# Channel groups of 28 contiguous channels, an output stored in two parts, and the D term on GpSimd, in an SSM kernel

## Chip, cores, metric

One core of one Trainium2 chip. The metric is device microseconds (us) of one execution; each kernel is timed in rounds beside the kernel before on the same chip. Profiles are of one execution; their span is some 1.8 us shorter than the time.

## The reference, cut to what matters

```python
x = A_u                                               # (1, 2048, 448), bf16
g = sigmoid((x * gate_w).sum(-1, keepdims=True))
a = S4(x)    # causal convolution of length 2048 with K[d,l] = Re sum_n C dB exp(dt A l), plus x * Dskip
b = x * (causal_conv(kv, ssm_k) + kv * ssm_D)         # kv = shift_conv(k) * v
return g * a + (1 - g) * b                            # (1, 2048, 448), bf16
```

Both convolutions are done as Fourier-like stages of small matmuls. The output is 2048 tokens of 448 channels; in memory one token is a row of 896 bytes.

## The kernel before

The 448 channels lie as 4 quarters (on partition groups of 32) of 112. A quarter is worked in four groups H = 0 to 3. Before, a group was 2 x 14 channels: 14 from each half of the quarter. Eight filter blocks (two for each group) build the S4 kernel K: products on VectorE, then 224 small matmuls into `pk`, an eviction `kg_S` (a copy out of the matmuls' accumulators by ScalarE), a gather, a spread. The products that the matmuls read are `kg_TP` and `kg_TQ`. All sums gather in `ug`, a tile of 128 x 64 x 112.

```python
def sk_cols(H, raw=None):                      # filter of B: D goes into its first tap
    raw = load_sk(H) if raw is None else raw   # 8 DMAs, one for each quarter and half
    s0 = raw[:, :, :, 0]
    V.tensor_tensor(out=s0, in0=s0, in1=dB[:].rearrange(...)[:, H * NW:(H + 1) * NW, :], op=ALU.add)
    return lambda h, w: raw[:, w, h, :]
...
def epilogue_B(H):                             # two multiplications of 448, one for each half
    ...
    for h in range(2):
        V.tensor_tensor(out=o[:, :, :, h], in0=pv[:, :, :, h], in1=o[:, :, :, h], op=ALU.mult)
...
def epilogue_A(H):
    ...
    V.tensor_tensor(out=o, in0=t, in1=o, op=ALU.add)           # the last sum of this group
    if H == NQG - 1:                                           # after the last group: whole rows
        for g in range(4):
            dmae[g % 2].dma_start(out4[g][:, b0:b0 + n, :], ug[g * 32:(g + 1) * 32, b0:b0 + n, :])
```

With halves interleaved, three finished groups were three times 14 columns at two places. So the output went out at the very end in whole quarter rows, 112 channels or 224 bytes at a time.

## Time and profile before

| | before |
|---|---|
| time, median of 3 | 339.62 us (339.61 to 339.71) |
| span of the profile | 338.0 us |
| last filter block's matmuls begin | 303.40 us |
| last sum on VectorE ends | 328.71 us |
| from there to the end ("tail") | 9.3 us |

The lines that carry this are in the prediction below. The view of the DMA queues in the stretch from 324 to 345 us (queue, packets, MB, share of 16 engines) shows the final stores:

```profile
q10 hardware_dynamic: 4224, 0.92, 26.9%
q1 hardware_dynamic: 4224, 0.92, 25.4%
```

From this comes a figure used throughout: 52.3% of 16 engines for 21 us, over 8448 packets, is **20.8 ns of packet time per packet** of 224 bytes. (A packet of the output is one run of contiguous bytes in a row: 2048 x 4 = 8192 of them, and 256 more.) It adds up the packets' own times. Where the engines are full these overlap, and the share passes 100% (119.6% from 329 to 335 us); the interval between two packets of an engine is then shorter, here 6 us x 16 / 5484 packets = 17.5 ns. And the timeline of TensorE (PE) in the last filter block (start, us, what, count, idle time before):

```profile
303.40 2.89 PE L367 MATMUL pk<-kg_TP,kg_TQ 128*21 128x32 bf16 x181
307.15 0.84 PE L367 MATMUL pk<-kg_TP,kg_TQ 128*21 128x32 bf16 x43 [0.87 <-issue]
```

The block's 224 matmuls are broken by a pause of 0.87 us for which the profile knows no releaser ("issue").

### The profile page before, as it was taken

To read this page: it belongs to the slowest core of one execution; us is meant where nothing else is said; L and a number is where in the kernel's file an instruction comes from. 1 tells how busy PE (TensorE), PEld (TensorE's weight loads), DVE (VectorE), ACT (ScalarE), POOL (GpSimd) and SP (SyncE) were. 2 spreads that over 40 slices of the span, in tenths; PEclk is the share of its full clock that TensorE was granted. 3 is DMA by queue.
4 is the path that set the end of the run, shared out by engine and by line. 5 is a ranking of instruction groups with operands and counts; after the bars stand their busy time and mean duration, and the time that the engine had idled before them with its cause. 6 is when DMAs were issued, how large, how long until landed. Compare 5 with 4: busy or idle time off the path is not lost.

```text
span 338.0 us, 12004 instructions
## 1 busy us (share of the span) xinstructions
PE 226.8 (67%) x5294; PEld 199.9 (59%) x5294; DVE 284.6 (84%) x610; ACT 237.5 (70%) x375; POOL 14.9 (4%) x132
## 2 busy tenths in 40 slices
PE   0098326686287448758897975997977769966740
PEld 0033226565286347748886864996966658965740
DVE  5799499798997999999979999796999999982440
ACT  4524368988996069997998998769889565942620
POOL 8700000000000000000000000000000000000000
PEclk9999677578559676987999995899878759977595
DMA  8899994422804000032004004100400120040039
GB/s 136 121 154 192 163 146 100 67 82 78 155 2 111 2 4 1 6 83 72 2 4 112 3 4 110 43 5 2 112 0 5 42 70 4 4 111 6 0 72 147
DMA packets 53803, 21.40 MB, mean 63 GB/s; under 512 B 49208, under 2 KB 52088, under 8 KB 53752
## 3 DMA queue, kind: packets, MB, share of 16 engines
q1 hardware_dynamic: 49064, 19.47, 31.6%
q10 hardware_dynamic: 4368, 1.03, 1.9%
q8 instruction: 41, 0.67, 0.8%
q0 software_dynamic: 320, 0.15, 0.3%
q14 instruction: 10, 0.08, 0.1%
HBM read 10.09 MB, written 3.21 MB: 39 GB/s over the span
## 4 chain that ended last, share of the span: by engine, by line
ACT 33%; PE 24%; DVE 19%; SPq 11%; DMA 7%; issue 4%; DVEq 0%; ACTq 0%
ACT zs L560 11%; PE ps_b L274 5%; PE pk L367 5%; ACT zsK L560 5%; PE ps_a L260 4%; PE ps_c L208 4%; ACT ET L479 4%; ACT U L560 4%; SPq L613 3%; DVE kg_P L313 2%; SPq L618 2%; ACT ET L491 2%; PE ps L221 2%; DMA modes<-in_A_C_im_dram 2%; ACT ks_mag L479 2%
## 5 line engine op out<-in xcount | busy, mean ns | idle before, releaser
L313 DVE TENSOR_TENSOR kg_P<-kg_TQ,ET 128x896 bf16<-128x896 bf16 (+1 forms) x64 | 43.8, 705 | 0.4
L221 PEld LDWEIGHTS <-s_W 128*128 128x128 bf16 x480 | 33.3, 117 | 17.5 <-issue 15.2
L560 ACT CAST zs<-ps_c 128x1024 bf16<-128x1024 f32 (+1 forms) x48 | 42.4, 936 | 0.6 <-PE ps_c L208 0.5
L560 ACT CAST zs<-ps 128x896 bf16<-128x896 f32 x48 | 40.9, 924 | 0.3 <-PE ps L221 0.2
L221 PE MATMUL ps<-zs,s_W 128*128 128x112 bf16 x384 | 31.0, 248 | 12.2 <-ACT zs L560 6.4
L260 PE MATMUL ps_a<-sa_R,zs 128*128 128x128 bf16 x196 | 30.4, 246 | 10.0 <-ACT zs L560 8.0
L491 ACT ACTIVATE ET<-ks_ph 128x448 bf16<-128x448 int16 x40 | 23.6, 604 | 16.2 <-DVE ks_ph L487 16.0
L560 ACT CAST zsK<-ps_c 128x512 bf16<-128x512 f32 (+2 forms) x30 | 25.6, 856 | 13.1 <-PE ps_c L208 13.1
L560 ACT CAST U<-ps_a 128x1024 bf16<-128x1024 f32 (+2 forms) x32 | 29.7, 948 | 4.9 <-PE ps_a L260 2.8
L367 PE MATMUL pk<-kg_TP,kg_TQ 128*21 128x32 bf16 x1792 | 29.4, 238 | 4.8 <-issue 3.8
L260 PEld LDWEIGHTS <-zsS 128*128 128x128 bf16 x196 | 26.8, 153 | 8.4 <-issue 8.1
L367 PEld LDWEIGHTS <-kg_TQ 128*21 128x21 bf16 x1792 | 27.6, 121 | 6.2 <-issue 5.6
L313 DVE TENSOR_TENSOR kg_P<-kg_TP,ET 128x1792 bf16<-128x1792 bf16 (+1 forms) x32 | 30.9, 965 | 0.0
L260 PE MATMUL ps_a<-sa_R,zsS 128*128 128x128 bf16 x196 | 30.2, 246 | 0.6 <-issue 0.6
L274 PE MATMUL ps_b<-U,sb_G 128*128 128x28 bf16 x1024 | 27.9, 177 | 3.4 <-ACT U L560 1.3
L274 PEld LDWEIGHTS <-sb_G 128*128 128x128 bf16 x1024 | 27.6, 98 | 4.1 <-issue 4.0
L661 PE MATMUL ps_v<-kvt,scratch 128*128 128x448 bf16 x64 | 17.1, 405 | 18.3 <-DVE kvt L657 17.9
L260 PEld LDWEIGHTS <-zs 128*128 128x128 bf16 x196 | 26.9, 153 | 3.4 <-DVE zs L281 2.0
L318 DVE TENSOR_TENSOR kg_TQ<-kg_P 128x896 bf16<-128x896 bf16 (+2 forms) x64 | 27.6, 441 | 0.2
L208 PE MATMUL ps_c<-WcK,kg_KT 128*64 128x128 bf16 x224 | 19.9, 303 | 10.3 <-ACT zsK L560 7.8
L208 PEld LDWEIGHTS <-kg_KT 128*64 128x64 bf16 x224 | 17.3, 209 | 12.1 <-issue 8.7
L661 PEld LDWEIGHTS <-scratch 128*128 128x128 bf16 x64 | 6.8, 108 | 28.1 <-issue 18.9
(138 smaller groups left out, 476.7 us busy)
## 6 DMA issues: line engine op xcount, KB each, us to landing
zsS<-zs SPq DMA_DIRECT2D x16, 448.0 KB, 4.4
kt<-in_B_k_dram SPq DMA_DIRECT2D x8, 224.0 KB, 5.9
vt<-in_B_v_dram SPq DMA_DIRECT2D x4, 448.0 KB, 8.2
skraw<-in_B_ssm_k_dram SPq DMA_DIRECT2D x32, 56.0 KB, 2.7
uu<-in_A_u_dram SPq DMA_DIRECT2D x4, 448.0 KB, 6.8
xfd<-ks_hold SPq DMA_DIRECT2D x2, 672.0 KB, 3.0
ks_xf<-xfd SPq DMA_DIRECT2D x3, 336.0 KB, 3.0
out_dram<-ug SPq DMA_DIRECT2D x8, 112.0 KB, 4.5
```

Source lines behind the costliest of these rows:

```text
L208: nc.tensor.matmul(pt[64 * r:64 * r + 64, i, :], lhsT=x, rhs=W[:, 128 * r:128 * r + 128], start=True, stop=True, tile_position=(0, 64 * r))
L221: nc.tensor.matmul(pt[:, i // 4, (i % 4) * n:(i % 4 + 1) * n], lhsT=W[:, k].rearrange("p r s -> p (r s)"), rhs=zs[:, k], start=True, stop= ...
L260: nc.tensor.matmul(pt[:, i, :], lhsT=t[:].rearrange("p k (g c) -> p (k g) c", g=4)[:, :, j + i], rhs=R[:, 128 * n:128 * n + 128], start=(n ...
L274: nc.tensor.matmul(o, lhsT=G[:, b, r].rearrange("p g a -> p (g a)"), rhs=U[:, r, b], start=(r == 0), stop=(r == 1))
L313: put(V.tensor_tensor(out=P4[:, i:i + m].rearrange("p n v c m -> p n v (c m)"), in0=in0, in1=in1, op=ALU.mult))
L318: put(V.tensor_tensor(out=T[:, dst:dst + v.shape[1] // 2].rearrange("p n v m -> p (n v) m"), in0=v[:, :, 0], in1=v[:, :, 1], op=ALU.add))
L367: nc.tensor.matmul(pt[32 * g:32 * g + NQ, hw, :].rearrange("p (i j) -> p i j", i=2), lhsT=TQ[:, :, c, m], rhs=rhs, start=(hf == 0 and c == 0),
L479: ex = nc.scalar.activation(dst, x, ACT.Exp, scale=float(e))
L491: sn = nc.scalar.activation(dst.rearrange("p b c m -> p b (c m)"), low16(ph[:].rearrange("p b c m -> p (b c m)")).rearrange("p (b x) -> p ...
L560: nc.scalar.copy(dst, src)
L613: nc.sync.dma_start(kt[g * 32:(g + 1) * 32, 3 + b0:35 + b0, :], k4[g][:, b0:b0 + 32, :])
L661: nc.tensor.matmul(pt[:, i, 0:448], lhsT=ident, rhs=t[:, n, 4 * i:4 * i + 4, :].rearrange("p b l -> p (b l)"), start=(n == 0), stop=(n == 3))
```

## The change

Its intent: a group is now 28 contiguous channels of a quarter. So three groups are columns 0 to 83, which can be stored while the last filter block is still being made, and only a quarter of the output is left for the end. Contiguous groups also make one operation of two in B's epilogue, and four DMAs of eight for the filter. The D term moves from VectorE to GpSimd, and priorities are set anew. Core of the diff:

```diff
     def sk_cols(H, raw=None):
         raw = load_sk(H) if raw is None else raw
-        s0 = raw[:, :, :, 0]
-        V.tensor_tensor(out=s0, in0=s0, in1=dB[:].rearrange("p (h v) -> p v h", h=2)[:, H * NW:(H + 1) * NW, :], op=ALU.add)
+        nc.gpsimd.tensor_tensor(out=raw[:, :, 0], in0=raw[:, :, 0], in1=dB[:, H * NC:(H + 1) * NC], op=ALU.add)
 ...
     def epilogue_B(H):
-            for h in range(2):
-                V.tensor_tensor(out=o[:, :, :, h], in0=pv[:, :, :, h], in1=o[:, :, :, h], op=ALU.mult)
+            V.tensor_tensor(out=o, in0=pt.rearrange("p i (b c) -> p i b c", b=16), in1=o, op=ALU.mult)
+    def store(b0, n, c0, c1):
+        for g in range(4):
+            dmae[g % 2 if c1 == 112 else 0].dma_start(out4[g][:, b0:b0 + n, c0:c1], ug[g * 32:(g + 1) * 32, b0:b0 + n, c0:c1])
     def epilogue_A(H):
+            if H == NQG - 2:
+                store(b0, n, 0, 3 * NC)
             if H == NQG - 1:
-                for g in range(4):
-                    dmae[g % 2].dma_start(out4[g][:, b0:b0 + n, :], ug[...])
+                store(b0, n, 3 * NC, 112)
 ...
-        with tc.high_priority(offset=200000):      # gather and spread of a filter block
+        with tc.high_priority(offset=100):
 ...
-        U = stage_a(nc, psum, qp, R, terms[c], evac)
+        with tc.high_priority(offset=300000):
+            U = stage_a(nc, psum, qp, R, terms[c], evac)
-        with tc.high_priority(offset=300000):      # stage B; the same for the products
+        with tc.high_priority(offset=200000):
```

(NC is 28, so 3 * NC is 84.)

More of the change, by code (lines that the diff above doesn't have):

```diff
@@ L21 @@
 HALF = 32768.0
-NV = 56
 NQG = 4
-NW = NV // NQG
-CW = 7
-NBLK = NV // CW
-M = 16 * CW
+NC = 112 // NQG
+CB = NC // 2
+NBLK = 2 * NQG
+M = 8 * CB
 NMODE = 896
@@ L199, in col_of, with spread @@
         return self.sel[:, self.var[key]].rearrange("p a b -> p (a b)")
-def spread(nc, psum, W, zs, cols, groups, evac, room=8, tag="ps", order=None):
+def spread(nc, psum, W, zs, cols, groups, evac, room=8, tag="ps", at=0):
     for whs in groups:
@@ L210, in spread @@
         n = len(whs)
-        at = order.index(whs[0]) if order else whs[0]
-        evac(zs[:].rearrange("p k (g c) -> p (k g) c", g=4)[:, :, at:at + n], pt[:, 0:n].rearrange("p i kg -> p kg i"))
+        evac(zs[:].rearrange("p k (g c) -> p (k g) c", g=4)[:, :, at + whs[0]:at + whs[0] + n], pt[:, 0:n].rearrange("p i kg -> p kg i"))
 def transform(nc, psum, W, zs, evac, ks=range(4)):
-    n = 8 * NW
+    n = 4 * NC
     for kk in ks:
@@ L238, in transform_half @@
             k0 = 16 * kk + 8 * i
-            evac(half_of(zs, k0, k0 + 8, half), pt[:, i, 0:448].rearrange("p (k c) -> p k c", c=NW), i)
+            evac(half_of(zs, k0, k0 + 8, half), pt[:, i, 0:448].rearrange("p (k c) -> p k c", c=CB), i)
 def stage_a_half(nc, psum, U, R, terms, evac, half):
-    for h in range(2):
+    for j in range(half * CB, half * CB + CB, 7):
         pt = psum.tile([P, 8, 128], f32, name="ps_a", tag="ps")
-        for i in range(CW):
+        for i in range(7):
             for n, t in enumerate(terms):
-                nc.tensor.matmul(pt[:, i, :], lhsT=t[:].rearrange("p k (g c) -> p (k g) c", g=4)[:, :, half * NW + h * CW + i],
+                nc.tensor.matmul(pt[:, i, :], lhsT=t[:].rearrange("p k (g c) -> p (k g) c", g=4)[:, :, j + i],
                                  rhs=R[:, 128 * n:128 * n + 128], start=(n == 0), stop=(n == 1))
-        j = h * NW + half * CW
-        evac(U[:, :, :, j:j + CW].rearrange("p r b c -> p (r b) c"), pt[:, 0:CW].rearrange("p i rb -> p rb i"))
+        evac(U[:, :, :, j:j + 7].rearrange("p r b c -> p (r b) c"), pt[:, 0:7].rearrange("p i rb -> p rb i"))
 def stage_a(nc, psum, pool, R, terms, evac):
-    U = pool.tile([P, 2, 64, 2 * NW], bf16, name="U", tag="q")
-    for j in range(0, 2 * NW, 8):
-        m = min(8, 2 * NW - j)
+    U = pool.tile([P, 2, 64, NC], bf16, name="U", tag="q")
+    for j in range(0, NC, 8):
+        m = min(8, NC - j)
         pt = psum.tile([P, 8, 128], f32, name="ps_a", tag="ps")
@@ L271, in stage_b @@
             b = b0 + i
-            o = pt[:, i // 16, (i % 16) * 2 * NW:(i % 16 + 1) * 2 * NW]
+            o = pt[:, i // 16, (i % 16) * NC:(i % 16 + 1) * NC]
             for r in range(2):
@@ L358, in block @@
             pt = self.pk[:, 0:448].rearrange("p (n b) -> p n b", b=32)
-            for hw in range(2 * CW):
-                h, w = divmod(hw, CW)
+            for hw in range(CB):
                 for hf in range(2):
@@ L363, in block @@
                         for g in range(4):
-                            m = ((hf * 4 + g) * 2 + h) * CW + w
+                            m = (hf * 4 + g) * CB + hw
                             r0 = TP[:, 0, c, m:m + 1]
@@ L369, in block @@
                                              stop=(hf == 1 and c == 1), tile_position=(0, 32 * g))
-            S = self.pool.tile([P, 32, 2 * CW], bf16, name="kg_S")
-            evac(S[:].rearrange("p b n -> p n b"), pt) if False else evac(S[:], pt.rearrange("p n b -> p b n"))
+            S = self.pool.tile([P, 32, CB], bf16, name="kg_S")
+            evac(S[:], pt.rearrange("p n b -> p b n"))
         return S
@@ L375, in gather @@
         nc, cons = self.nc, self.cons
-        KT = self.pool.tile([P, 64, 2, CW], bf16, name="kg_KT")
+        KT = self.pool.tile([P, 64, CB], bf16, name="kg_KT")
         for r in range(8):
@@ L401, in gather @@
             if r == 0:
-                for h in range(2):
-                    v0 = h * NV + j * CW
-                    jobs.append((0, o[0:32, 0, h * CW:(h + 1) * CW], self.sel_d[:], self.d4[:, v0:v0 + CW]))
+                jobs.append((0, o[0:32, 0, :], self.sel_d[:], self.d4[:, j * CB:(j + 1) * CB]))
             for a0 in range(4):
@@ L411, in gather @@
             if r % 4 == 3:
-                evac(KT[:].rearrange("p (b r) h w -> p r b (h w)", r=8)[:, r - 3:r + 1], pt[:, 0:448].rearrange("p (r b n) -> p r b n", r=4, b=8))
+                evac(KT[:].rearrange("p (b r) n -> p r b n", r=8)[:, r - 3:r + 1], pt[:, 0:448].rearrange("p (r b n) -> p r b n", r=4, b=8))
         return KT
@@ L429, in scaled @@
         for i, t in enumerate(self.hold):
-            nat = lambda ap: ap.rearrange("p f (x b w) -> p f x b w", x=8, w=CW)[:, :, :, 4 * i:4 * i + 4]
+            nat = lambda ap: ap.rearrange("p f (g b w) -> p f g b w", g=4, w=CB)[:, :, :, 4 * i:4 * i + 4]
             dtv = self.dt[:].unsqueeze(1).to_broadcast([P, 2, 448])
-            self.nc.vector.tensor_tensor(out=dst(t).rearrange("p b (f x w) -> p f x b w", f=2, w=CW), in0=nat(src), in1=nat(dtv), op=ALU.mult)
+            self.nc.vector.tensor_tensor(out=dst(t).rearrange("p b (f g w) -> p f g b w", f=2, w=CB), in0=nat(src), in1=nat(dtv), op=ALU.mult)
     @staticmethod
@@ L575, in hqt @@
         return qp.tile(shape, dtype, name=name, tag="hq", bufs=NBH)
-    sk_src = B_ssm_k.rearrange("(g h v) (a b) -> g h a v b", g=4, h=2, a=32)
+    sk_src = B_ssm_k.rearrange("(g c) (a b) -> g a c b", g=4, a=32)
     def load_sk(H):
-        raw = hqt([P, NW, 2, 64], "skraw")
+        raw = hqt([P, NC, 64], "skraw")
         for g in range(4):
-            for h in range(2):
-                nc.sync.dma_start(raw[g * 32:(g + 1) * 32, :, h, :], sk_src[g, h][:, H * NW:(H + 1) * NW, :])
+            nc.sync.dma_start(raw[g * 32:(g + 1) * 32], sk_src[g][:, H * NC:(H + 1) * NC, :])
         return raw
@@ L587, in sk_cols, with spread_in @@
         raw = load_sk(H) if raw is None else raw
-        s0 = raw[:, :, :, 0]
-        V.tensor_tensor(out=s0, in0=s0, in1=dB[:].rearrange("p (h v) -> p v h", h=2)[:, H * NW:(H + 1) * NW, :], op=ALU.add)
-        return lambda h, w: raw[:, w, h, :]
-    halves = [h * NW + s * CW + w for s in range(2) for h in range(2) for w in range(CW)]
-    def spread_in(cols, order=None):
-        zs = qt([P, 32, 8 * NW], "zs")
-        groups = [(order or list(range(2 * NW)))[j:j + 8] for j in range(0, 2 * NW, 8)]
-        spread(nc, psum, Wc, zs, lambda wh: cols(*divmod(wh, NW)), groups, evac, order=order)
+        nc.gpsimd.tensor_tensor(out=raw[:, :, 0], in0=raw[:, :, 0], in1=dB[:, H * NC:(H + 1) * NC], op=ALU.add)
+        return lambda c: raw[:, c, :]
+    def spread_in(cols):
+        zs = qt([P, 32, 4 * NC], "zs")
+        spread(nc, psum, Wc, zs, cols, [list(range(j, min(j + 8, NC))) for j in range(0, NC, 8)], evac)
         return zs
@@ L601, in with_swap @@
         transform(nc, psum, W2, zs, evac)
-        swap = qt([P, 32, 8 * NW], "zsS")
+        swap = qt([P, 32, 4 * NC], "zsS")
         for r in range(2):
@@ L671, in body @@
     for H in range(NQG):
-        q = lambda t: t.rearrange("p b (h v) -> p b h v", h=2)[:, :, :, H * NW:(H + 1) * NW]
-        kvq.append(hqt([P, 64, 2, NW], "kv"))
+        q = lambda t: t[:, :, H * NC:(H + 1) * NC]
+        kvq.append(hqt([P, 64, NC], "kv"))
         kvl = V.tensor_tensor(out=kvq[H][:], in0=q(vt[:]), in1=q(kt[:, 3:67]), op=ALU.mult)
@@ L708, in block @@
         if KA[H] is None:
-            KA[H] = qt([P, 32, 8 * NW], "zsK")
+            KA[H] = qt([P, 32, 4 * NC], "zsK")
         S = kg.block(j, evac, kvl if j == 0 else None)
-        with tc.high_priority(offset=200000):
+        with tc.high_priority(offset=100):
             KT = kg.gather(j, S, evac)
-            w0 = (j % 2) * CW
-            groups = [[h * NW + w0 + w for w in range(CW)] for h in range(2)]
-            cols = lambda wh: KT[:, :, wh // NW, wh % NW - w0]
+            at = (j % 2) * CB
+            cols = lambda c: KT[:, :, c]
@@ L716, in block @@
             if j == NBLK - 1:
-                spread(nc, psum, WcK, KA[H], cols, groups, evac, order=halves)
+                spread(nc, psum, WcK, KA[H], cols, [range(0, 7), range(7, 14)], evac, at=at)
             else:
-                spread(nc, psk, WcK, KA[H], cols, [x for q in groups for x in (q[0:4], q[4:])], evac, 4, "ps_g",
-                       halves if H == NQG - 1 else None)
+                spread(nc, psk, WcK, KA[H], cols, [range(0, 4), range(4, 8), range(8, 11), range(11, 14)], evac, 4, "ps_g", at)
@@ L722, in window @@
     def window(b0, n, H):
-        return ug[:, b0:b0 + n, :].rearrange("p (i b) (h v) -> p i b h v", b=16, h=2)[:, :, :, :, H * NW:(H + 1) * NW]
+        return ug[:, b0:b0 + n, H * NC:(H + 1) * NC]
     def epilogue_B(H):
         def consume(b0, n, pt):
-            o = window(b0, n, H)
-            pv = pt.rearrange("p i (b h w) -> p i b h w", b=16, h=2)
-            for h in range(2):
-                V.tensor_tensor(out=o[:, :, :, h], in0=pv[:, :, :, h], in1=o[:, :, :, h], op=ALU.mult)
-        return consume
+            o = window(b0, n, H).rearrange("p (i b) c -> p i b c", b=16)
+            V.tensor_tensor(out=o, in0=pt.rearrange("p i (b c) -> p i b c", b=16), in1=o, op=ALU.mult)
@@ L733, in epilogue_A @@
+        return consume
+    def store(b0, n, c0, c1):
+        for g in range(4):
+            dmae[g % 2 if c1 == 112 else 0].dma_start(out4[g][:, b0:b0 + n, c0:c1], ug[g * 32:(g + 1) * 32, b0:b0 + n, c0:c1])
     def epilogue_A(H):
         def consume(b0, n, pt):
-            t = kgp.tile([P, 2, 16, 2, NW], bf16, name="ept")
-            t = t[:, 0:n // 16]
-            V.tensor_tensor(out=t.rearrange("p i b h w -> p i b (h w)"), in0=pt.rearrange("p i (b x) -> p i b x", b=16),
-                            in1=gt[:, b0:b0 + n].rearrange("p (i b) -> p i b", b=16).unsqueeze(3).to_broadcast([P, n // 16, 16, 2 * NW]), op=ALU.mult)
@@ L739, in consume @@
-            o, t = [x.rearrange("p i b h w -> p (i b) h w") for x in (window(b0, n, H), t)]
-            V.tensor_tensor(out=o, in0=t, in1=o, op=ALU.add)
+            t = kgp.tile([P, 32, NC], bf16, name="ept")[:, 0:n]
+            V.tensor_tensor(out=t.rearrange("p (i b) c -> p i b c", b=16), in0=pt.rearrange("p i (b c) -> p i b c", b=16),
+                            in1=gt[:, b0:b0 + n].rearrange("p (i b) -> p i b", b=16).unsqueeze(3).to_broadcast([P, n // 16, 16, NC]), op=ALU.mult)
+            V.tensor_tensor(out=window(b0, n, H), in0=t, in1=window(b0, n, H), op=ALU.add)
@@ L741, in consume @@
+            if H == NQG - 2:
+                store(b0, n, 0, 3 * NC)
             if H == NQG - 1:
-                for g in range(4):
-                    dmae[g % 2].dma_start(out4[g][:, b0:b0 + n, :], ug[g * 32:(g + 1) * 32, b0:b0 + n, :])
+                store(b0, n, 3 * NC, 112)
         return consume
     def kv_cols(H):
-        return lambda h, w: kvq[H][:, :, h, w]
+        return lambda c: kvq[H][:, :, c]
     def u_cols(H):
-        return lambda h, w: uu[:, :, h * NV + H * NW + w]
+        return lambda c: uu[:, :, H * NC + c]
@@ L757, in step @@
         else:
-            XA[H] = spread_in(u_cols(H), halves if H == NQG - 1 else None)
-        U = stage_a(nc, psum, qp, R, terms[c], evac)
+            XA[H] = spread_in(u_cols(H))
+        with tc.high_priority(offset=300000):
+            U = stage_a(nc, psum, qp, R, terms[c], evac)
         if kind == "B":
@@ L764, in step @@
             XA[H] = with_swap(XA[H])
-        with tc.high_priority(offset=300000):
+        with tc.high_priority(offset=200000):
             stage_b(nc, psum, G, U, (epilogue_A if c[0] == "A" else epilogue_B)(c[1]))
         if kind == "B":
-            with tc.high_priority(offset=300000):
+            with tc.high_priority(offset=200000):
                 terms[n] = products(nc, *KB[H], XB[H])
@@ L774, in step @@
             transform(nc, psum, W2, KA[H], evac)
-            with tc.high_priority(offset=300000):
+            with tc.high_priority(offset=200000):
                 terms[n] = products(nc, *XA[H], KA[H])
@@ L797, in body @@
         step(seq[j], seq[j + 1], j)
-    U = qt([P, 2, 64, 2 * NW], "U")
+    U = qt([P, 2, 64, NC], "U")
     def last(half):
```

## The prediction

> **What bounds the kernel now.** I read the page's busy table and its row of slices first, then the waits of VectorE (DVE), then the chain that ended last in order of time, and last the timeline of the end.
>
> ```profile
> PE 226.8 (67%) x5294; PEld 199.9 (59%) x5294; DVE 284.6 (84%) x610; ACT 237.5 (70%) x375; POOL 14.9 (4%) x132
> ...
> DVE  5799499798997999999979999796999999982440
> ACT  4524368988996069997998998769889565942620
> ```
>
> DVE is at nine tenths or more in nearly every slice up to about 304 us. Its few idle gaps are these (engine and line waited for: us in total, times, longest):
>
> ```profile
> DVE ept L737 <- PE ps_b L274: 7.9, 4, 4.5
> DVE ET L503 <- ACT ET L491: 6.8, 4, 3.0
> DVE skraw L589 <- DMA skraw<-in_B_ssm_k_dram: 6.7, 2, 4.3
> ```
>
> So the kernel has three parts. Up to about 90 us, loads and DVE alternate, with 6.7 us in which DVE stands in front of its own 28-element add (the D term) because the filter's load has not landed. From 90 to 303 us DVE is nearly full, but after 196 us the chain of waits no longer names it: it runs over ACT evictions and PE, so DVE and the PE-ACT pair are both close to the bound. From 303.4 us on, all is one serial chain (last filter block, gather, spread, transform, two stages, output). The chain (start, us, what) and the end of the timeline:
>
> ```profile
> 29.67 7.12 DMA modes<-in_A_C_im_dram
> 36.81 3.23 DMA skraw<-in_B_ssm_k_dram
> ...
> 62.15 2.90 DMA skraw<-in_B_ssm_k_dram
> 65.72 1.85 DVE ks_tC_im L456
> ```
>
> ```profile
> 325.27 7.69 SPq L743 DMA_DIRECT2D out_dram<-ug  x8
> 325.28 8.10 ACTq L743 DMA_DIRECT2D out_dram<-ug  x8
> ...
> 328.32 0.39 DVE L740 TENSOR_TENSOR ug<-ept,ug 128x448 bf16<-128x448 bf16 x1
> ```
>
> The last arithmetic ends at 328.71 and the span at 338.0: 9.3 us are output stores alone.
>
> **What the Trainium skill says.** (1) "DMA: Bandwidth & Descriptors", section "Why small descriptors are slow (HBM only)": each packet carries a fixed overhead on the engine's internal bus, beside its 32-byte beats, and fixed descriptor metadata. The trace agrees in kind: in windows with the 16 DMA engines full, 128-byte packets ran at 119 GB/s (36 to 37 us), 224-byte ones at 155 (28 to 29) and 512-byte ones at 234 (34 to 35), which is 17, 23 and 35 ns per packet and engine. A straight line through these has some 11 ns at zero bytes: a 56-byte packet costs an estimated 14 ns, not a quarter of 23. (2) "VectorE: DVE Perf Modes", section "Why PSUM operands drop a tier": a float32 PSUM operand goes at one element per cycle. Agrees: 896 elements from PSUM took 1086 ns (L737), 448 took 616 (L730), so a fixed part of about 146 ns. (3) "GPSIMD Engine Reference", section "Key points": GpSimd shares its SBUF interfaces with VectorE and is about half as fast at elementwise work. No two-input GpSimd operation is in this trace, so nothing here shows it. (4) "ScalarE: Activation LUTs", section "What ACT_TABLE_LOAD costs": about 1283 ns for the load. Agrees: 1283 ns in every row of table loads, 13 of them.
>
> **The change, part by part.**
>
> *D added on GpSimd.* Four DVE adds go: 4 x 0.284 = 1.1 us. The wait is another matter. The second of the two waits (2.37 us at 63.1, in front of L456) should vanish: in the changed order DVE has ks_tC_im next, whose PSUM operand was written by 60.3. The first (4.30 us at 36.0) should not. In the changed order of instructions GpSimd's first add stands in front of three of the four sb_j iotas, and DVE's next operation needs the second iota, which in the kernel before was made at 14.07, long ahead. So the new wait is load, add, iota (0.62 us each in the timeline), then DVE. The load itself is a little earlier: before, the eighth skraw DMA waited for a transfer slot that modes C_im freed at 36.79, after which 3.23 us passed, and in 38 to 39 us the DMA share fell to 0.71; now four DMAs of twice the size need slots freed sooner. The bytes stay behind the same modes bytes, so I take 0.5 us off the landing at 40.04. Then an add (0.5 us, an estimate from GpSimd's 0.2 us for small memsets and 0.65 for iotas) and an iota: sb_ph starts near 40.8 instead of 40.41. The new order also has only one of two phases ahead of the first four mask products, which delays the second sine; I count +1.0 us for this stage in all.
>
> *Epilogue of B in one piece.* 16 instructions of 616 ns become 8 of 1086 (the same shape as L737 now): 9.9 - 8.7 = 1.2 us less on DVE.
>
> *Order around the gate.* The changed order on ACT has 12 table loads instead of 13: the sine that stood after the gate's sigmoid is now before it. Before, DVE waited 1.69 us at 84.7 for just that sine: -1.7 us.
>
> *Priorities.* Stage A goes ahead of the gather, the gather behind. The order on PE and DVE is otherwise close to the old one, and PE's tail after the last filter block is the same. One place looks worse: before the last block, the second-to-last block's spread had 8 of its 28 matmuls ahead of stage B (292.05), now all 28 follow it. They go through one PSUM buffer, and a round of matmul and eviction took 1.5 to 1.7 us there (297.06, 298.45, 300.21). One more round after stage B, less about 0.8 us that stage A gains by not being broken up: +0.8 us, on the path to the last block's matmuls.
>
> *Smaller things.* One D-skip matmul per block instead of two (8 fewer, 0.2 us each at most), half as many skraw DMAs at the same packets: nothing on the path.
>
> *Output.* Columns 0 to 83 go out after the third A epilogue, whose sums ended at 299.7 and 302.8. Eight DMAs on the SP queue with 1024 packets each, 8192 x 20 ns / 16 = 10 us from 300: landed near 313, behind nothing that matters (the last swap was issued at 296), 12 us before the queue is needed. The final stores keep their 16 DMAs and 8192 packets, but of 56 bytes. Before: 512 packets per engine, from 325.6 to about 336.7, 21.7 ns each: DMA-bound. Now 512 x 14 = 7.2 us if full, and the sums that feed them come every 1.15 us until 328.7, so at best the last four DMAs start at 329 and land in the 2.9 us that the fastest store took. I take the last landing at 332.5 instead of 337: -4.5 us. This is the largest and surest term.
>
> **Sum.** DVE before the last block: +1.0 - 2.4 - 1.1 - 1.2 - 1.7 = -5.4 us. Since the chain after 196 us runs over ACT and PE, I let 60% of it through: -3.2. Spread order: +0.8. Stores: -4.5. In all -6.9: 339.6 - 6.9 = 332.7, I say 332.6.
>
> **The rivals.**
> 1. *The stores cost by the packet, not the byte.* The final part has as many packets as before; if a 56-byte write costs HBM as much as a 224-byte one, the tail stays at 9 us and the result is about 337. Against it: reads show 17 ns at 128 bytes and 23 at 224. For it: no store below 224 bytes is in the trace.
> 2. *PE and ACT are the bound after 90 us.* Then the DVE savings come back as DVE idle time, and only stores and some of the start remain: 339.6 - 4.5 + 0.8 - 1 = 335. For it: the chain after 196 us. Against: DVE had under 6 us of idle time between 130 and 303.
> 3. *DVE savings come through in full and the new priorities clear PE and ACT waits* (stage A sooner means U, stage B and buffers sooner): -5.4 - 4.5 and 1 or 2 more: 328.5. For it: eviction and PE waits of 8 to 13 us in total (kg_S, zsK, ps_a) that priorities can move.
> 4. *GpSimd holds things up*: its add could be blocked by DVE's two-input work, or its wait in front of the iotas be longer than I count. Then the start loses 2 or 3 us and the result is near 335.5. Slower than before by 2% would need a stall of 13 us, and nothing in the order points to one.
>
> **Range and chances.** The stores may give 1 to 5.5, DVE 1 to 6, priorities -2 to +2, the start -1 to +2; combined about 3 us to each side, a little more upwards: 328.5 to 337. The 2% line is 332.8, just about my value; the priorities look tuned for this layout, which tips it a little: 0.52 faster, 0.46 within, 0.02 slower.
>
> **What would show it.** Right: the time from the last DVE sum to the end is 5 us or less; no DVE wait on a skraw DMA, but one of 4 to 5 us on GpSimd's iota near 36 us; DVE near 281 us busy; 12 table loads; the last block's matmuls (pk) start some 2 us earlier than 303.4. Wrong: final stores still taking 9 us (rival 1); DVE idle between 90 and 300 us grown by the 3 to 4 us that it saved (rival 2); DVE waiting more than 6 us for GpSimd (rival 4).

## The result

The changed kernel took **344.19 us** in the median of 4 runs (343.67 to 345.17), the kernel before in the same rounds 339.66 (339.61 to 340.61). The ratio is 1.013, 95% interval 1.010 to 1.016: slower, by less than the 2% line. Ratios here are the mean time of one kernel's fast runs over that of the other's fast runs of the same rounds, so not quite the ratio of the medians quoted.

The busy row of the page after (busy us, share, instructions):

```profile
PE 224.7 (66%) x5286; PEld 196.2 (57%) x5286; DVE 284.6 (83%) x598; ACT 233.1 (68%) x374; POOL 16.9 (5%) x136
```

VectorE has 12 instructions fewer and is busy for the same 284.6 us. The last sum in the timeline after:

```profile
328.50 0.39 DVE L727 TENSOR_TENSOR ug<-ept,ug 128x448 bf16<-128x448 bf16 x1
```

The last sum ends at 328.50 + 0.39 = 328.89, where before it ended at 328.71: the arithmetic is no faster. The tail is 342.1 - 328.89 = 13.2 us, where before it was 9.3. A quarter of the bytes takes 3.9 us longer, nearly the whole difference of the spans (4.1). The DMA queues from 324 to 345 us:

```profile
q10 hardware_dynamic: 4224, 0.23, 45.5%
q1 hardware_dynamic: 4224, 0.23, 35.8%
```

The same 8448 packets, a quarter of the megabytes, and 81.3% x 16 x 21 us / 8448 = **32.3 ns per packet**. The prediction had 14, as an interval between packets of full engines; measured in that way it is 8 us x 16 / 4327 packets = 29.6 ns (330 to 338 us). The early store, whose packets of 168 bytes are the only large traffic between 298 and 318 us, shows the same:

```profile
q1 hardware_dynamic: 8322, 1.38, 81.1%
```

81.1% x 16 x 20 us / 8322 = 31.2 ns per packet, more than the 20.8 of the longer 224 bytes.

These are means of two very different stretches. Two views of one microsecond each, from 327 and from 329 us:

```profile
q1 hardware_dynamic: 722, 0.04, 41.2%
q10 hardware_dynamic: 632, 0.03, 33.3%
```

```profile
q10 hardware_dynamic: 387, 0.02, 144.8%
q1 hardware_dynamic: 280, 0.02, 68.0%
```

So the first packets of 56 bytes took 8.8 ns each (74.5% x 16 us / 1354), and two microseconds later 51.0 (212.8% x 16 us / 667). The early store does it too (17 ns a packet from 299 to 301 us, 30 to 54 from 302 to 309), and so do the misaligned stores of split_72 and split_76 below, each after some 2300 to 3400 packets; the aligned ones do not (split_80 has 9.2, 10.5, 11.0, 11.0 and 12.2 ns in the five microseconds from 327). Why, no run shows. And TensorE in the last filter block:

```profile
301.17 3.12 PE L363 MATMUL pk<-kg_TP,kg_TQ 128*21 128x32 bf16 x191
307.24 0.71 PE L363 MATMUL pk<-kg_TP,kg_TQ 128*21 128x32 bf16 x33 [2.96 <-issue]
```

The block starts 2.2 us earlier than before, as predicted ("some 2 us earlier than 303.4"), but its pause has grown from 0.87 to 2.96 us. So the block ends where it did, and the eviction that follows starts at 308.00 where it was 308.03. (The start of this block varies: in seven later kernels with the same order of arithmetic it lay between 301.9 and 304.6, in one execution each, so these 2.2 us are not a sure gain either.)

Two of the waits of VectorE after, both near the start (us in total, times, longest):

```profile
DVE sb_ph L87 <- POOL sb_j L138: 3.6, 1, 3.6
DVE sb_G L147 <- ACT sb_v L144: 3.6, 2, 2.8
```

No wait for skraw is left: both, 6.7 us, are gone. New are 3.6 us for GpSimd's iota and more waits for the sine behind it. The timeline of GpSimd shows why:

```profile
39.60 0.32 POOL L581 TENSOR_TENSOR skraw<-skraw,dB 128x28 bf16<-128x28 bf16 x1 [25.55 <-DMA skraw<-in_B_ssm_k_dram]
39.80 1.14 POOL L138 IOTA sb_j<- 128x512 int32 x2
43.33 0.77 POOL L138 IOTA sb_j<- 128x512 int32 x1 [2.38 <-DVE sb_ph L87]
```

The add waits for the load, and the iotas, of which two wait for nothing, stand behind it. The k-v product starts at 51.62, 2.8 us later than before (48.80); 0.8 us of these were lost before the add (VectorE's `kvt` products start at 17.12, before at 16.28). The gains that follow (no second skraw wait, no wait for a table load) just make up for it: the first filter block's products start at 89.61, before at 89.74.

Two suspects, then: what the two stores do (tail and pause), and why nothing else in the change gained.

### The profile page after: what moved, and what is told of

Its sections match the earlier page's. It is cut to its first block, busy times and chain, and to the rows that moved or that the text cites. A ratio compares the mean times of both kernels' runs of the same rounds, so it can differ in the third digit from the quotient of the medians.

```text
span 342.1 us, 11970 instructions
## 1 busy us (share of the span) xinstructions
PE 224.7 (66%) x5286; PEld 196.2 (57%) x5286; DVE 284.6 (83%) x598; ACT 233.1 (68%) x374; POOL 16.9 (5%) x136
## 3 DMA queue, kind: packets, MB, share of 16 engines
HBM read 10.09 MB, written 3.21 MB: 39 GB/s over the span
## 4 chain that ended last, share of the span: by engine, by line
ACT 33%; PE 27%; DVE 19%; SPq 10%; issue 4%; DMA 3%; DVEq 0%; POOL 0%; ACTq 0%; POOLq 0%
ACT zs L554 11%; PE pk L363 8%; PE ps_b L271 6%; PE ps_c L207 5%; ACT zsK L554 5%; PE ps_a L257 4%; ACT U L554 4%; ACT ET L473 3%; SPq L602 3%; ACT ET L485 2%; SPq L607 2%; ACT ks_mag L473 2%; DVE kg_P L310 2%; PE ps L219 2%; SPq L613 2%
## 5 line engine op out<-in xcount | busy, mean ns | idle before, releaser
L219 PEld LDWEIGHTS <-s_W 128*128 128x128 bf16 x480 | 30.8, 110 | 19.3 <-issue 17.1
L363 PE MATMUL pk<-kg_TP,kg_TQ 128*21 128x32 bf16 x1792 | 29.6, 238 | 13.3 <-DVE kg_TP L320 8.3
L219 PE MATMUL ps<-zs,s_W 128*128 128x112 bf16 x384 | 28.9, 234 | 14.2 <-ACT zs L554 9.0
L554 ACT CAST U<-ps_a 128x1024 bf16<-128x1024 f32 (+2 forms) x32 | 28.9, 940 | 6.5 <-PE ps_a L257 4.6
L554 ACT CAST zsK<-ps_c 128x512 bf16<-128x512 f32 (+2 forms) x30 | 22.5, 756 | 13.2 <-PE ps_c L207 13.2
L650 PE MATMUL ps_v<-kvt,scratch 128*128 128x448 bf16 x64 | 17.8, 414 | 19.0 <-DVE kvt L646 18.7
```

Source lines behind the costliest of these rows:

```text
L219: nc.tensor.matmul(pt[:, i // 4, (i % 4) * n:(i % 4 + 1) * n], lhsT=W[:, k].rearrange("p r s -> p (r s)"), rhs=zs[:, k], start=True, stop= ...
L363: nc.tensor.matmul(pt[32 * g:32 * g + NQ, hw, :].rearrange("p (i j) -> p i j", i=2), lhsT=TQ[:, :, c, m], rhs=rhs, start=(hf == 0 and c == 0),
L554: nc.scalar.copy(dst, src)
L650: nc.tensor.matmul(pt[:, i, 0:448], lhsT=ident, rhs=t[:, n, 4 * i:4 * i + 4, :].rearrange("p b l -> p (b l)"), start=(n == 0), stop=(n == 3))
```

## The experiments

Twelve kernels ran, in three groups on one chip each, all but shift_fetch in rounds with the kernel before. "Cut" is the column at which the output is divided between early and final store. Since a quarter row begins at a multiple of 224 bytes in rows of 896 bytes, both multiples of 32, a run is aligned to 32 bytes exactly if twice the cut is a multiple of 32. (In the built program `ug` lies at byte 29,984 of each partition, a multiple of 32 too. So a cut is aligned or not on both sides at once, in on-chip memory where the store reads and in HBM where it writes, and no run here tells the two apart.)

### 1. No early store: late_store

```diff
-            if H == NQG - 2:
-                store(b0, n, 0, 3 * NC)
-                store(b0, n, 3 * NC, 112)
+                store(b0, n, 0, 112)
```

> The changed kernel without the early store; the final stores carry all 112 channels (224-byte runs) again. The order of instructions on PE, DVE and GpSimd is the changed kernel's. Theory A (short misaligned runs make the final stores slow: 13.2 us from the last sum to the end, against 9.3 before): the tail goes back to 9.3. Theory B (the early store's 8192 packets hold up PE's instruction fetch, which is the 2.96 us gap in the last block's pk matmuls): the gap falls to about 1 us, so the last sum comes 2 us earlier, near 326.8. A and B: span 336, 338 us in time. A without B: span 338.2, time 340. Rival (the tail is long because the queue's transfer slots are still held by the early store): tail 9.3 here too, told apart by early_and_full.

Measured: 339.91 us (338.38 to 341.47), ratio to before 0.9995 (0.9951 to 1.0039). Last sum at 329.42, tail 9.4 us, and the pause:

```profile
303.57 3.06 PE L363 MATMUL pk<-kg_TP,kg_TQ 128*21 128x32 bf16 x191
307.92 0.71 PE L363 MATMUL pk<-kg_TP,kg_TQ 128*21 128x32 bf16 x33 [1.29 <-issue]
```

What follows: the whole loss is the divided store. And all the rest of the change (grouping, GpSimd, one-piece epilogue, priorities) is worth nothing in sum, within 0.5% either way; gains and losses may cancel in it.

### 2. Early store kept, and whole rows at the end: early_and_full

```diff
-                store(b0, n, 3 * NC, 112)
+                store(b0, n, 0, 112)
```

The result is the same (columns 0 to 83 are written twice with the same values).

> The changed kernel with its early store kept, and the final stores again of all 112 channels, so that 84 are written twice with the same values. Theory A (run length or alignment): tail 9.3 us from the last sum, as before the change. Rival (the early store's slots or its traffic make the tail long): tail stays near 13. Theory B (instruction fetch behind the early store): the gap of some 3 us in the last pk matmuls stays, last sum near 328.9. So A and B: span 338.2, time 340; rival: time 344.

Measured: 342.25 us, ratio 1.006 (1.0021 to 1.0098). Tail 9.4 us. The order of the instructions on every compute engine is that of late_store, yet the last sum ends at 331.49, 2.07 us later:

```profile
303.92 3.24 PE L363 MATMUL pk<-kg_TP,kg_TQ 128*21 128x32 bf16 x183
307.55 0.40 PE L363 MATMUL pk<-kg_TP,kg_TQ 128*21 128x32 bf16 x8 [0.39 <-issue]
310.00 0.71 PE L363 MATMUL pk<-kg_TP,kg_TQ 128*21 128x32 bf16 x33 [2.05 <-issue]
```

What follows: with whole rows at the end the long tail is gone, so it belongs to the 56-byte runs. The early store is what lengthens the pause: 0.39 + 2.05 = 2.44 us against 1.29 for the same instructions without it. (One profile each; the ratios' intervals overlap by a little.)

### 3. The cut at a multiple of 32 bytes: split_80

```diff
-                store(b0, n, 0, 3 * NC)
+                store(b0, n, 0, 80)
-                store(b0, n, 3 * NC, 112)
+                store(b0, n, 80, 112)
```

160 bytes early and 64 at the end. Number and kind of DMAs, packets and order of instructions are those of the changed kernel.

> The changed kernel with the cut between early and final stores at channel 80 in place of 84: early runs of 160 bytes, final runs of 64, both starting and ending on multiples of 32 bytes; as many packets as the changed kernel. If it is alignment that costs (a run that covers part of a 32-byte unit needs a read first): the final stores get quicker than those of before, 15 ns a packet or less, tail 6 to 7 us, span 335, and the early store lands in less than its 8.9 us median. If it is short runs as such: 64 bytes are hardly better than 56, tail 12 to 13 us, time 343.

Measured: **336.65 us** (336.2 to 337.73), ratio 0.9904 (0.9875 to 0.9932). The last sum, then the DMA queues from 324 to 345 us:

```profile
328.76 0.39 DVE L727 TENSOR_TENSOR ug<-ept,ug 128x448 bf16<-128x448 bf16 x1
```

```profile
q10 hardware_dynamic: 4224, 0.26, 14.9%
q1 hardware_dynamic: 4224, 0.26, 13.7%
```

28.6% x 16 x 21 us / 8448 = 11.4 ns per packet, and a tail of 334.9 - 329.15 = 5.75 us. Four columns moved from one store to the other turn 32 ns into 11, and 13.2 us of tail into 5.75. The pause is 1.62 us. What follows: packets as such are cheap (that ends rival 1 of the prediction), those of 64 bytes too. Whether the 56-byte runs are dear for their length or because they do not keep to 32 bytes was to be parted by the next cuts.

### 4. Other cuts: split_76, split_72, split_64

The edit is as in split_80, with 76, 72 and 64 in place of 80.

> Control for the cut at 80: the cut at channel 76. Final runs of 72 bytes, longer than the 64 of the cut at 80, but their start, and the end of the early runs of 152, lies 24 bytes into a 32-byte unit. Alignment theory: as slow as the cut at 84, tail 12 to 13 us, early store landing in 7 to 9 us, time 343 to 344. If it is length that costs below 64 bytes: tail under 6 us as with the cut at 80, time 336 to 337.

> The changed kernel with the cut at column 72: runs of 144 bytes early and 80 bytes at the end, all starts and lengths multiples of 16 bytes but not all of 32. If what counts is whole 32-byte units, it behaves as the cuts at 76 and 84 did: a tail of about 12 us, landings of 6 to 9 us, about 344 to 347 us. If 16 bytes are enough, it behaves as the cut at 80: a tail of about 6 us, about 337 us.

> The cut at column 64: 128 bytes early, 96 bytes at the end, all multiples of 32. If aligned runs cost by a line through 64 bytes (tail 5.75 us) and 224 bytes (9.4 us), the tail is about 6.5 us and the time about 337.5. If aligned runs cost the same per packet whatever their length up to 96 bytes, the tail is 5.8 and the time about 336.7. If alignment was not the cause in the cut at 80 but its early columns, the tail is nearer 10.

Measured: 347.47, 345.78 and 336.89 us; ratios 1.0215 (1.0154 to 1.0275), 1.0156 (1.0105 to 1.0208) and 0.9892 (0.9842 to 0.9943). The DMA queues of split_72 from 324 to 345 us, and of split_64 from 324 to 336 us:

```profile
q10 hardware_dynamic: 4224, 0.33, 44.8%
q1 hardware_dynamic: 4224, 0.33, 37.5%
```

```profile
q10 hardware_dynamic: 4224, 0.39, 32.1%
q1 hardware_dynamic: 4224, 0.39, 29.3%
```

For split_72 that is 82.3% x 16 x 21 / 8448 = 32.7 ns, for split_64 61.4% x 16 x 12 / 8448 = 13.9 ns. All cuts together, each worked out in this way:

| kernel | final run, bytes | multiple of 32 | final, ns per packet | early run, ns per packet | tail, us | pause, us | ratio to before |
|---|---|---|---|---|---|---|---|
| after (84) | 56 | no | 32.3 | 168 B: 31.2 | 13.2 | 2.96 | 1.013 |
| split_76 | 72 | no | 34.7 | 152 B | 12.7 | 2.79 | 1.0215 |
| split_72 | 80 | no, of 16 | 32.7 | 144 B: 32.8 | 13.0 | 2.65 | 1.0156 |
| split_80 | 64 | yes | 11.4 | 160 B | 5.75 | 1.62 | 0.9904 |
| split_64 | 96 | yes | 13.9 | 128 B: 15.2 | 6.5 | 1.92 | 0.9892 |
| late_store | 224 | yes | 20.8 | none | 9.4 | 1.29 | 0.9995 |

(An early figure is left out where another large transfer lies in the same stretch. Split_80 ran again in 6.) What follows: length is not it, since 72 and 80 bytes cost three times what 64 does, and 96 bytes is cheap again. Sixteen bytes are not enough: split_72 keeps to 16 and pays in full. With whole units of 32 bytes the cost follows a line: through 64 and 224 bytes (11.4 and 20.8 ns) it gives 13.3 for 96 bytes, measured 13.9; the expected tail of 6.5 us was met. That alignment to 32 bytes decides is shown. Why is not, nor on which side of the transfer. The Trainium skill, "Collectives: The Full Stack", section "Rules for kernel authors", says of buffers that 32-byte alignment prevents a read-modify-write in hardware. The step at 32 bytes agrees with such a thing. But the profile's count of HBM reads is 10.09 MB for every kernel here, so no run shows the reading itself. And a cost that every packet pays at once would not fit the fast first packets (see the result).

### 5. What the pause is: shift_fetch

In all kernels with the new order, the pause stood after the 191st matmul of the last block, whatever VectorE did. Either it belongs to a place in TensorE's program, or the data for the next matmul came late.

```diff
+        if b0 == 16:
+            for i in range(48):
+                nc.tensor.matmul(pt[:, 0, 0:32], lhsT=ident, rhs=t[:, 3, 0, 0:32], start=True, stop=True)
         for i in range(2):
             for n in range(4):
```

48 matmuls early in the kernel, overwritten by the real ones that follow: 96 rows (weight load and matmul) more in TensorE's program.

> The changed kernel with 48 harmless extra matmuls early on TensorE (32 columns each, overwritten by the real ones); nothing else in the order of the engines' instructions changes but for those rows, each matmul being two rows (a weight load and a product). Theory place in the program: the pause of TensorE in the last filter block comes at a fixed row of its program, so it moves from after the 191st of the 224 matmuls to after about the 143rd (between 140 and 146), and the smaller pauses in the second and fifth blocks move by 48 matmuls as well, from 58 to about 106 and from 4 to about 52 before the block's end. Rival, place in the data: TensorE waits there for the last table products, and the pause stays after the 191st. Time in both: 343.5 to 346.

Measured, first the changed kernel in its fourth block, then shift_fetch in its fourth and its last:

```profile
200.22 3.49 PE L363 MATMUL pk<-kg_TP,kg_TQ 128*21 128x32 bf16 x220
204.78 0.24 PE L363 MATMUL pk<-kg_TP,kg_TQ 128*21 128x32 bf16 x4 [1.06 <-issue]
```

```profile
200.20 2.74 PE L363 MATMUL pk<-kg_TP,kg_TQ 128*21 128x32 bf16 x172
204.21 0.95 PE L363 MATMUL pk<-kg_TP,kg_TQ 128*21 128x32 bf16 x52 [1.27 <-issue]
...
307.25 2.39 PE L363 MATMUL pk<-kg_TP,kg_TQ 128*21 128x32 bf16 x143
312.87 1.44 PE L363 MATMUL pk<-kg_TP,kg_TQ 128*21 128x32 bf16 x81 [3.23 <-issue]
```

The pause of the last block moved from after 191 to after 143, to the matmul; in the fourth block 4 matmuls before the end became 52. A place in the program is shown. (The third pause foretold, 106 before the end of the first block, did not show; my expectation also called these blocks the second and the fifth, but counted right they are the first and the fourth.) Counting weight loads and matmuls, the rows of TensorE's program in each built kernel, the row at which each pause over 0.4 us in a filter block stands is:

```
before       1715  2739  5295  9899
after        1721  5299  9905
prio_80      1721  3765  5299  6323  7601  8625  9649  9905
shift_fetch  2743  4021  5299  6579  7857  8881  9905
remainder by 256: 171 to 185 for every one
```

The pauses stand on a grid of 256 rows. (If TensorE's 24 to 29 semaphore and control rows are counted too, the remainder is 193 or 194 for every one.) Not every crossing shows one: the eight blocks cross the grid 12 to 15 times, with 3 to 8 such pauses. The page of every kernel has this line among its DMA queues:

```profile
q8 instruction: 41, 0.67, 0.8%
```

41 packets of 16 KB; TensorE's program has some 10,570 rows, and 41 times 256 is 10,496. So a packet is 256 rows, the spacing of the pauses. That a pause stands exactly where one packet ends is inferred: no view says which rows a packet holds. The Trainium skill, "Runtime: NRT & Kernel Launch", section "Terms", says that an engine's instruction memory is refilled in 16 KiB blocks. The trace agrees, and adds the price: a pause of up to 1.5 us when the DMA engines are nearly idle (a share of 0.03 around that longest one, in shift_fetch's third block), 1.6 to 1.9 us while an aligned early store is under way, 2.0 to 3.2 us while a misaligned one is. That the refill waits behind the store's packets is the natural reading, but it is inferred: no view shows one packet waiting for another. What can be read is the refill's packet that starts last before the pause of the last block: it took 1.12 us itself in late_store and 1.83 in the changed kernel (its share in a window of 0.25 us, times 16 engines), 0.7 of the 1.7 us by which the pause grew. (With misaligned stores under way there are also pauses of 0.2 to 0.5 us off the grid; I have no account of them.)

This kernel took 352.35 us in its one run (343.5 to 346 were expected), 8 us more than the changed kernel, for 48 short matmuls. The waits of TensorE in the filter blocks, first after, then shift_fetch:

```profile
PE pk L363 <- issue: 5.0, 3, 3.0
```

```profile
PE pk L363 <- issue: 10.0, 7, 3.2
```

The pauses in the filter blocks grew by five us (10.0 from 5.0). Since it is one run, I take it as a hint only: where the grid falls in a program can matter more than the instructions added.

### 6. GpSimd, priorities, and the rest of the gain: iota_first, prio_80, prio_iota_80, dve_80, split_80_b

iota_first is the changed kernel (cut 84) with the add kept behind the second iota:

```diff
-        nc.gpsimd.tensor_tensor(out=raw[:, :, 0], ...)
+        ad = nc.gpsimd.tensor_tensor(out=raw[:, :, 0], ...)
+        if H == 0:
+            after(tc, ad, cons.iota2)
```

> The changed kernel with one order forced: GpSimd's first D add stands behind the second sb_j iota, not ahead of it. The order on PE and ACT in the first 50 us is then that of the kernel before. Theory (the add in front of the iotas, and the filter's matmuls in front of the last seven ps_v matmuls, cost the start 2.8 us: kv at 51.6 against 48.8): kv near 47 to 48, since DVE no longer waits for the load at all; first kg_P of the filter blocks 2 to 4 us ahead of 89.6. Whether that reaches the end: if DVE is the bound, up to 3 us off 344.2; if PE and ACT are, or the gap in the last pk matmuls eats it, 344 again. The tail stays at 13 us.

prio_80 is split_80 with the priorities of before (gather 200000, stage A none, stage B and products 300000):

> The cut at 80 with the priorities of the kernel before (gather 200000, stage A none, stage B and products 300000). If the new priorities cost the middle of the kernel time (first kg_P of the blocks were 1.4 to 2 us late at 140 to 257 us): 1 to 2 us faster than the cut at 80 alone, 335. If they are what made pk of the last block start 2 us sooner: 1 to 2 us slower, 338.5. If priorities hardly matter here: 336.7.

prio_iota_80 is both:

> The same old priorities, the cut at 80, and GpSimd's first add behind the second iota. The start gains 5 us on VectorE (first kg_P of block 0 near 85 against 90.5). If the loss of iota_first in the middle (first kg_P 5.4 us early until 151 us, but the last sum 2 us late) came from the order that the scheduler made with the new priorities: 332 to 334 us. If VectorE's head start is worth nothing because PE and ScalarE bound the middle: 337 or more.

dve_80 is split_80 with the D term on VectorE again (`V.tensor_tensor` for `nc.gpsimd.tensor_tensor`):

> The cut at 80 with the D add on VectorE as before. The start is that of the kernel before: one wait of some 4 us for the load, another of 2, kv near 49. If the move to GpSimd with its order cost the start 2.8 us and gained the second wait back: level with the cut at 80, 336 to 337.5. If the move itself is a gain beyond that: 338 to 339.

split_80_b is split_80 once more, with 5 rounds:

> The cut at column 80 once more, word for word the kernel of the run split_80, for a narrower interval: 336.7 plus or minus 0.7, a ratio to the kernel before of 0.988 to 0.995. If its first result was a lucky chip, the ratio is 0.995 to 1.

Measured:

| kernel | time, us | ratio to before (95%) | first block's products start | last block's matmuls start |
|---|---|---|---|---|
| iota_first | 346.64 | 1.0191 (1.0162 to 1.0221) | 85.13 | 304.25 |
| prio_80 | 336.81 | 0.9925 (0.9866 to 0.9984) | 89.16 | 300.43 |
| prio_iota_80 | 338.61 | 0.9972 (0.9916 to 1.0027) | 85.53 | 304.63 |
| dve_80 | 338.85 | 0.9971 (0.9921 to 1.0021) | 88.84 | 305.82 |
| split_80_b | 337.06 | 0.9899 (0.9857 to 0.9941) | 90.64 | 302.01 |

With the iotas first, VectorE starts the filter blocks over 4 us earlier than in the changed kernel (89.61), and the last block starts no sooner for it. Where did the lead go? On the way VectorE waits longer for the chain of TensorE and ScalarE: for the swapped tile zsS, a transfer of what these two have made, it waits 8.7 us in prio_iota_80, in the changed kernel 1.9.

```profile
DVE zsS L280 <- DMA zsS<-zs: 8.7, 3, 4.9
```

But some of the lead arrives. TensorE and VectorE just before the last block in prio_iota_80:

```profile
298.81 1.65 PE L235 MATMUL ps<-zsK,s_W 128*128 128x56 bf16 x32 [0.97 <-ACT zsK L556]
304.63 3.06 PE L365 MATMUL pk<-kg_TP,kg_TQ 128*21 128x32 bf16 x191 [4.17 <-DVE kg_TP L322]
...
300.81 0.63 DVE L796 TENSOR_TENSOR zsS<-zsS,zsK 128x896 bf16<-128x896 bf16 x1 [1.96 <-ACT zsK L556]
...
303.49 1.09 DVE L322 TENSOR_TENSOR kg_TP<-kg_TP,ET 128x1792 bf16<-128x1792 bf16 x1
```

TensorE is free at 300.46, earlier than the last block starts in any kernel with the changed order (301.17 to 304.56). It then stands 4.17 us for the last `kg_TP`, because in VectorE's program this product now stands behind five other operations (zsS, zs, ug, zsS, zs), the first of which waits for ScalarE. In the changed kernel and in every cut of it, it stands ahead of the four zsS and zs (in split_80 at 300.37). iota_first (TensorE free at 300.07) and dve_80 (at 301.65) have this other order and the same wait of 4.17 us; in all three, the order of the instructions changed on every engine, beyond what the edit asked for. So these runs do not show that a lead of VectorE is worth nothing: part of it was lost to the chain of TensorE and ScalarE, as rival 2 of the prediction has it, and the rest to an order in which VectorE itself came last. What a lead is worth with the order kept was not tested.

The priorities of before and of the change come to the same within these intervals (0.9925 beside 0.9904 and 0.9899): prio_80 starts the last block earlier, but interleaves it with other work and has pauses of 1.24 and 1.88 us in it. With the D term on VectorE the ratio is 0.9971, on GpSimd 0.9904 and 0.9899; intervals touch, the groups ran on different chips, and dve_80 has the 4.17 us wait, so whether GpSimd gains anything stays open. The repeat holds split_80: 1.0% faster than before, twice. It, split_64 (0.9892) and prio_80 (0.9925) beat both kernels.

## Why the prediction was wrong

The prediction was 332.6 us, its range 328.5 to 337; measured 344.2. It gave "slower by over 2%" two in a hundred and no thought to slower by 1.3%.

1. **The stores, "the largest and surest term": -4.5 us predicted.** This is the step that failed. Measured by late_store (ratio 0.9995) against after (1.013), the divided store costs 1.35%, some +4.6 us: 9 us off, of a miss of 11.6. It failed in the packet's cost: 14 ns by a line through *loads* of 128, 224 and 512 bytes, measured 29.6 in the same way (32.3 by packet time). For aligned stores the line is on the safe side: it gives 14 ns at 64 bytes and 16 at 96, measured 11.4 and 13.9. What it left out is that all its points were multiples of 32 bytes and the point it was used for, 56, was not; and that a packet's cost need not be a constant (8.8 ns at first, 51.0 two us later). Done with an aligned cut, the same idea gives a tail of 5.75 us (foretold: "5 us or less") and 3.3 us less than late_store on the same chip.
2. **"behind nothing that matters" for the early store.** Wrong too. 10 us were predicted for it; it was under way from about 299 to 313 us, so it lies over the whole last filter block, and lengthens TensorE's pause there by some 1 to 2 us. I looked only for other data transfers in its way, not at the queue of instructions.
3. **"I let 60% of it through: -3.2", and +0.8 for the order of the spread.** Together -2.4; late_store shows -0.2 (0.9951 to 1.0039, so -1.7 to +1.3). Its parts came mostly as said: adds gone, epilogue shorter, second skraw wait gone, table loads 12 instead of 13, GpSimd's iota a wait of 3.6 us where 4 to 5 were foretold. But the start lost 2.8 us, not 1.0: 0.8 before the add, the rest as the iotas stood behind the add one after the other and the sines behind them. So VectorE came to the filter blocks with no lead at all (89.61, before 89.74), and the 60% had nothing to let through. Rival 2 is likely right in part: of the 4.5 us that iota_first had at its first block, TensorE was ahead by 1.1 at the last one (free at 300.07, in the changed kernel 301.17; one profile each). Its sign was in the page: I saw that the chain after 196 us ran over ACT and PE, and still gave VectorE most of the weight because it had "under 6 us of idle time between 130 and 303". That reading was wrong: it was busy for 161.9 of these 173 us, and its named waits there come to 10.5. (The list of its gaps also leaves out the longest, 10.2 us for ScalarE's zsK in the serial end.)
4. **VectorE "near 281 us busy": 284.6.** The 1.1 us of adds went. The epilogue of B took 1.2 us less by the sum of its durations, as predicted, but only 0.5 us less of busy time (9.2 to 8.7), because the short instructions had overlapped. In the first 15 us VectorE was busy for 0.7 us more (11.06, before 10.36): one small constant of 128 elements took 2.90 us, before 0.27, and two of a single column 2.67 on average, before 0.14; these ran side by side, and another (s_ph) took less in turn. The other 0.9 us I have not traced, and none of this was tested.
5. **The rivals.** Rival 1 was near in its outcome (a tail that stays long) and wrong in its reason: cost by the packet. Aligned packets cost by length plus a fixed part (11.4 ns at 64 bytes, 20.8 at 224); misaligned ones of 56 to 168 bytes took 31 to 35 ns in the mean whatever their length. Rival 4 (GpSimd holds up) was right in kind for the start, at 2 of the 2.8 us. Rival 3 fell.

## What to carry to other kernels

Before dividing a store, work out the byte address of the cut: the short runs of these stores were cheap where both ends kept to 32 bytes, and two to three times as dear where not, so move the cut to the nearest aligned column even though a finished group is then a little larger than what is sent. Read a straight line through measured packets only for packets of the same alignment. And when the chain that ends last has left an engine, do not count that engine's savings by its full row; test once with a lead, and first compare the order of the instructions in both programs, since a scheduler that moves one product can cost as much as the lead gave (4.17 us here).

## What the Trainium skill lacked or had wrong

- "DMA: Bandwidth & Descriptors": its section "Specifications" puts a read-modify-write at transfers under 512 bytes, and its account of small packets (cited in the prediction) has no cost of 32-byte alignment. Here all runs were under 512 bytes, and alignment parted them: 32.3, 34.7 and 32.7 ns per packet at 56, 72 and 80 bytes, against 11.4 and 13.9 at 64 and 96. An alignment rule of 32 bytes that names a read-modify-write stands only in "Collectives: The Full Stack", for other buffers. No page has that the first 2300 to 3400 misaligned packets go fast (8.8 ns at 56 bytes) before the rest slow down (51.0).
- "Runtime: NRT & Kernel Launch": its section "Instruction fetch mechanics" has the refill in blocks of 256 instructions and calls the cost of crossing a block "mostly hidden". Here TensorE paused at some of the crossings, 0.4 to 1.5 us each in filter blocks with quiet DMA engines and up to 3.2 us while a store of many short packets ran.
- "GPSIMD Engine Reference": its measured add of two inputs is of a large tile, and small ones scatter: four adds of 128 x 28 bf16 took 0.32, 0.54, 0.57 and 0.72 us in the changed kernel, where VectorE took 0.284, and one each in iota_first and prio_iota_80 took 5.81 and 5.89 (spans on GpSimd are rough).
